# Sign of decoded weights by a parametric ReLU on ScalarE, and the feed-forward weights' low parts subtracted on VectorE: what it does to a one-core attention and gated-MLP kernel

## The chip, the cores and the metric

The kernel runs on one core of a Trainium2 chip. The metric is the device time of one execution in microseconds. A profile of one execution is at hand; its engines are TensorE (PE, and PEld for its weight loads), VectorE (DVE), ScalarE (ACT), GpSimd (POOL) and SyncE (SP), which here only issues DMAs.

## The reference, cut to what matters

All inputs are float64 in the host's arrays; the chip gets their bits and makes float32 of them.

```python
# attention in chunks of 64 tokens, batch 8, heads 8, 576 tokens, head_dim 64
attn = softmax(q_c @ k_c.T / 8) @ v_c
x = attn_out as (8, 576, 512)
# gated stage
gate = sigmoid(causal 5-tap depthwise convolution of x with conv_w)
x = (gate * (x @ w_val)) @ w_out
# feed-forward stage
xn = (x - mean) / sqrt(var + 1e-6) * g_ln
out = x + max(xn @ w_ch1, 0) @ w_ch2        # w_ch1 512x2048, w_ch2 2048x512
```

## The kernel before, in words

Tokens (4608) go in nine blocks of 512. The first stage runs attention and the gated stage block by block (`period`, in an order written out by hand for PE, DVE and ACT) and stores its result `y` in DRAM. The second stage first takes block 0 alone through the feed-forward layer (`ff1`, `ff2`, one step for each of the 16 slices f of 128 hidden columns), while the feed-forward weights are being loaded and decoded; after that the other eight blocks go in pairs (`ff_pair`, lines 597 to 660), with sums of weight slices that `make_pair` prepares.

Every matrix product is made of float32r operands in two parts, a high part and a low part, so each weight tile of 128x512 is needed as `hi` and `lo`. How a weight tile is made (`split`, line 103): the float64 tile is loaded into `raw` as two 32-bit words per number. `decode_copy` (line 87, ACT) reads the high words as if they were float32, multiplies by 2^-112 and writes `a` (tile `da`). `decode_bits` (DVE) shifts `a` left by 3 bits (line 91), which pushes the sign and the top exponent bits out, puts the sign bit of the high word back (line 92, inputs `raw` and `a`), and puts the top 3 bits of the low word in (line 93, inputs `raw` and `a`). `parts` makes `hi` as a copy of `a` rounded to float32r (line 100, ACT) and `lo` as `a - hi` (line 101, POOL).

There are 41 decodes: the convolution weights (20x128), four tiles of `w_val` and four of `w_out` in the first 60 us (`split_w`), and 32 tiles of `w_ch1` and `w_ch2`, two for each f (`split_ff`, called from `early_ff` for f below 4 and from `next_ff`, interleaved with `ff1` and `ff2`, for the rest). `ff_copy`, `ff_bits` and `ff_parts` (lines 709 to 722) are defined and never called. Tile `da` has three buffers in each of two pools, `raw` two in each; a tile of `raw` is free for the next load when line 93 has read it. For f of `w_ch1` the decoded tile is also stored to DRAM (line 147).

In the second stage only PE's order is written by hand; the order on DVE, ACT, POOL and SP is laid out by a planner ahead of time, from priorities and estimated durations, and each engine then works through its own list in order. On DVE the other work of that stretch is the low part `hl` of the hidden layer (line 455), layer norm (`ln_rows`, lines 411 to 423) and, at its end, the operands of the pairs (`right_operands`, lines 478 and 546). ACT has `hh` (line 454), the normalised rows (line 425), the evictions of transposes (line 435) and four square roots (line 416) beside lines 87 and 100.

Of the kernel before, what the change touches and what calls it, by code (L numbers as in the profile page):

```python
# [8 lines left out]
F32 = mybir.dt.float32  # L9
F32R = mybir.dt.float32r  # L10
U32 = mybir.dt.uint32
ACTF = mybir.ActivationFunctionType
ALU = mybir.AluOpType
# [6 lines left out]
def tile_chunk_attention_gated_mlp(ctx: ExitStack, tc: tile.TileContext, qk, v, w_val, conv_w, w_out, g_ln, w1, w2, out):  # L20
    nc = tc.nc
# [22 lines left out]
    scale = 1.0 / float(D) ** 0.5  # L44
# [39 lines left out]
        nc.sync.dma_start(out=t.rearrange("p c h d -> p (c h d)"), in_=v[u])  # L84

    def decode_copy(raw, a):
        nc.scalar.activation(out=a, in_=raw[:, :, 1].bitcast(F32), func=ACTF.Copy, scale=2.0 ** -112)

    def decode_bits(raw, a):
        lw, hw, au = raw[:, :, 0], raw[:, :, 1], a.bitcast(U32)  # L90
        nc.vector.tensor_scalar(out=au, in0=au, scalar1=3, scalar2=None, op0=ALU.logical_shift_left)
        nc.vector.scalar_tensor_tensor(out=au, in0=hw, scalar=0x80000000, in1=au, op0=ALU.bitwise_and, op1=ALU.bitwise_or)  # L92
        nc.vector.scalar_tensor_tensor(out=au, in0=lw, scalar=29, in1=au, op0=ALU.logical_shift_right, op1=ALU.bitwise_or)  # L93

    def decode(raw, a):
        decode_copy(raw, a)
        decode_bits(raw, a)

    def parts(hi, lo, a):
        nc.scalar.activation(out=hi, in_=a, func=ACTF.Copy)  # L100
        nc.gpsimd.tensor_tensor(out=lo, in0=a, in1=hi, op=ALU.subtract)  # L101

    def split(hi, lo, raw, pool=None):
        a = (pool or stg).tile([P, DM], F32, tag="da", name="da", bufs=3)
        decode(raw, a)
        parts(hi, lo, a)
        return a

    wv = {}
# [8 lines left out]
    def split_w(nm, c0=0, c1=CT):  # L118
        hs, ls = wv.setdefault(nm + "s", ([], []))
        for c, raw in list(enumerate(wv[nm]))[c0:c1]:  # L120
            hi = pD1.tile([P, DM], F32R, name=f"{nm}h{c}")
            lo = pD1.tile([P, DM], F32R, name=f"{nm}l{c}")
            split(hi, lo, raw)
            hs.append(hi)
            ls.append(lo)
# [13 lines left out]
    def split_ff(f, pool):  # L139
        r1, r2 = wraw.pop(f)  # L140
        g, m = divmod(f, NFA)
        if g in (0, 3):
            t = wA.tile([P, 2, DM], F32R, tag=f"s{NFA + m}", name="w0")
        else:
            t = p2[f"w{g}"].tile([P, 2, DM], F32R, tag=f"w{m}", name="w0")
        a = split(t[:, 0, :], t[:, 1, :], r1, pool)
        nc.sync.dma_start(out=a_dram[f], in_=a)
        w1s[f] = (t[:, 0, :], t[:, 1, :])
        t = (wA if f < NFA else p2["w"]).tile([P, 2, DM], F32R, tag=f"s{f}" if f < NFA else f"w1_{f}", name="w1")
        split(t[:, 0, :], t[:, 1, :], r2, pool)  # L150
        w2s[f] = (t[:, 0, :], t[:, 1, :])


# [555 lines left out]
    def ff_copy(k):  # L709
        a = fa[k] = stg.tile([P, DM], F32, tag="da", name="da", bufs=3)  # L710
        decode_copy(wraw[k // 2][k % 2], a)

    def ff_bits(k):
        decode_bits(wraw[k // 2][k % 2], fa[k])

    def ff_parts(k):
        f, a = k // 2, fa.pop(k)
        t = wA.tile([P, 2, DM], F32R, tag=f"s{f if k % 2 else NFA + f}", name="w1" if k % 2 else "w0")
        parts(t[:, 0, :], t[:, 1, :], a)
        (w2s if k % 2 else w1s)[f] = (t[:, 0, :], t[:, 1, :])  # L720
        if k % 2 == 0:
            nc.sync.dma_start(out=a_dram[f], in_=a)

    def early_ff(f):
        load_ff(f, stg)
        split_ff(f, stg)
# [194 lines left out]
    def next_ff(f):  # L921
        if NE <= f < NF:
            pool = stg2 if f % 2 else stg
            load_ff(f, pool)
            split_ff(f, pool)
# [95 lines left out]
```

## Time and profile before

| | |
|---|---|
| median of three runs | 1103.33 us (1102.24 to 1105.18) |
| profiled execution, its time | 1105.21 us |
| profiled execution, span of its instructions | 1103.4 us |
| PE busy | 1058.8 us (96%), granted clock 0.989 of full |
| DVE busy | 698.6 us (63%) |
| ACT busy | 499.6 us (45%) |
| POOL busy | 106.2 us (10%), of which line 101 57.8 us |
| chain that ended last | PE 79%, DVE 12%, ACT 3%, DMA 3% |

The 1.8 us between the profiled execution's time and its span lie around the instructions. Engine shares are means over the whole span; the stages differ, so the rows below take single stretches, in microseconds from the start of the span. The feed-forward weights are decoded from about 287 to 403 us.

### The profile page before, as it was taken

What the parts mean: (1) busy time and instruction counts of PE and PEld (TensorE: products, weight loads), DVE (VectorE), ACT (ScalarE), POOL (GpSimd) and SP (SyncE); (2) the same over time, 40 slices, a digit from 0 to 9 for tenths busy, and PEclk for the clock granted to TensorE, in tenths of its full rate; (3) what the DMA queues carried; (4) which work ended last, traced back from release to release, by engine and by line L of the source; (5) the groups of instructions that cost most, each with busy time, mean ns of one, the idle gap of its engine ahead of it and who ended that gap; (6) DMA issues with size and microseconds to landing.
All of it is one profiled execution on the core that took longest, in us unless ns stands there. A gap on an engine that the chain in (4) does not pass through costs nothing.

```text
span 1103.4 us, 16877 instructions
## 1 busy us (share of the span) xinstructions
PE 1058.8 (96%) x6778; PEld 862.9 (78%) x6778; DVE 698.6 (63%) x1107; ACT 499.6 (45%) x872; POOL 106.2 (10%) x120
## 2 busy tenths in 40 slices
PE   4899999999899898999999999999999999999998
PEld 3578888888677676888888888888888888888887
DVE  5899999997969987556638335448334447433434
ACT  5777777776756654344433233433233323222221
POOL 1210000000124444222200000000000000000000
PEclk9999999999999898999999999999999999999999
DMA  9534344412387745333335523323533224522211
GB/s 374 204 140 144 136 144 154 144 59 78 115 280 234 240 162 219 134 116 134 135 136 167 173 96 115 117 93 125 200 103 108 97 85 132 194 94 96 77 39 76
DMA packets 58725, 156.32 MB, mean 142 GB/s; under 512 B 5758, under 2 KB 13974, under 8 KB 56214
## 3 DMA queue, kind: packets, MB, share of 16 engines
q1 hardware_dynamic: 58646, 155.23, 40.7%
q8 instruction: 53, 0.87, 0.3%
q14 instruction: 26, 0.21, 0.1%
HBM read 117.46 MB, written 37.75 MB: 141 GB/s over the span
## 4 chain that ended last, share of the span: by engine, by line
PE 79%; DVE 12%; ACT 3%; DMA 3%; issue 2%; POOL 1%; SPq 0%; ACTq 0%; DVEq 0%; POOLq 0%
PE x L610 16%; PE acc L584 16%; PE psf L584 15%; PE zy L610 9%; PE pso L335 8%; PE psv L335 8%; PE sc L175 2%; PE x L250 2%; DVE da L92 2%; DVE h L622 2%; PE pst L218 1%; DMA qkr<-in_qk 1%; DVE da L93 1%; PE pst L433 1%; DVE xt L546 1%
## 5 line engine op out<-in xcount | busy, mean ns | idle before, releaser
L630 DVE TENSOR_TENSOR c<-x,c 128x512 f32<-128x512 f32 x96 | 66.2, 690 | 235.5 <-ACT c L626 179.6
L584 PE MATMUL acc<-w,h 128*128 128x512 f32 x768 | 184.5, 390 | 0.0
L584 PE MATMUL psf<-w,h 128*128 128x512 f32 x768 | 184.3, 389 | 0.0
L584 PEld LDWEIGHTS acc<-w,h 128*128 128x128 f32 x768 | 144.3, 188 | 30.1
L584 PEld LDWEIGHTS psf<-w,h 128*128 128x128 f32 x768 | 144.3, 188 | 29.8
L610 PE MATMUL x<-t,wc 128*128 128x512 f32 x576 | 149.0, 395 | 4.6 <-DVE c L630 4.6
L626 ACT ACTIVATE c<-zy 128x512 f32<-128x512 f32 x96 | 57.8, 602 | 185.2 <-PE zy L610 185.1
L610 PEld LDWEIGHTS x<-t,wc 128*128 128x128 f32 x576 | 109.3, 190 | 28.8 <-DVE c L630 6.2
L621 ACT ACTIVATE h<-c 128x512 fp32r<-128x512 f32 x96 | 60.6, 631 | 134.8 <-DVE c L630 134.2
L589 DVE TENSOR_TENSOR yt<-psf,yt 128x512 f32<-128x512 f32 x128 | 88.1, 690 | 23.5 <-PE psf L584 20.7
L304 DVE SCALAR_TENSOR_TENSOR cg<-xf,cw,cg 128x516 f32<-128x516 f32 (+1 forms) x136 | 100.4, 752 | 3.0
L610 PE MATMUL zy<-b,wc 128*128 128x512 f32 x384 | 99.1, 394 | 0.0
L610 PEld LDWEIGHTS zy<-b,wc 128*128 128x128 f32 x384 | 71.7, 189 | 14.4
L622 DVE SCALAR_TENSOR_TENSOR h<-c,h 128x512 fp32r<-128x512 f32 x96 | 68.0, 708 | 11.2 <-ACT h L621 10.9
L335 PE MATMUL pso<-oh,gh 128*128 128x512 f32 x144 | 58.3, 405 | 1.8 <-ACT gh L371 1.8
L335 PE MATMUL psv<-xh,vh 128*128 128x512 f32 x144 | 59.2, 411 | 0.0
L335 PE MATMUL pso<-oh,gl 128*128 128x512 f32 x144 | 56.9, 395 | 1.9 <-DVE gl L374 1.9
L101 POOL TENSOR_TENSOR w<-da,w 128x512 fp32r<-128x512 f32 x32 | 46.1, 1447 | 114.7 <-ACT w L100 108.7
L335 PE MATMUL pso<-ol,gh 128*128 128x512 f32 x144 | 56.6, 393 | 0.0
L335 PE MATMUL psv<-xl,vh 128*128 128x512 f32 x144 | 56.6, 393 | 0.0
L335 PE MATMUL psv<-xh,vl 128*128 128x512 f32 x144 | 56.6, 393 | 0.0
L621 ACT ACTIVATE h<-x 128x512 fp32r<-128x512 f32 x32 | 19.2, 598 | 81.3 <-PE x L610 81.3
(114 smaller groups left out, 1591.9 us busy)
## 6 DMA issues: line engine op xcount, KB each, us to landing
wc<-wc SPq DMA_DIRECT2D x112, 512.0 KB, 3.2
qkr<-in_qk SPq DMA_DIRECT2D x19, 1024.0 KB, 7.4
raw<-in_moe_w_ch SPq DMA_DIRECT2D x32, 512.0 KB, 4.4
vr<-in_v SPq DMA_DIRECT2D x18, 512.0 KB, 4.2
yd<-y SPq DMA_DIRECT2D x36, 256.0 KB, 2.0
out<-yt SPq DMA_DIRECT2D x36, 256.0 KB, 3.7
yr<-yd SPq DMA_DIRECT2D x32, 256.0 KB, 3.2
yt<-yd SPq DMA_DIRECT2D x32, 256.0 KB, 3.7
```

Source lines behind the costliest of these rows:

```text
L92: nc.vector.scalar_tensor_tensor(out=au, in0=hw, scalar=0x80000000, in1=au, op0=ALU.bitwise_and, op1=ALU.bitwise_or)
L101: nc.gpsimd.tensor_tensor(out=lo, in0=a, in1=hi, op=ALU.subtract)
L175: nc.tensor.matmul(out=ps[CH * c:CH * c + CH, par, g, :], lhsT=qt[r0:r0 + CH, hp, cs], rhs=kt[r0:r0 + CH, hp, cs], start=True, stop=True,)
L304: last_tap[j] = nc.vector.scalar_tensor_tensor(out=o, in0=xf[j][:, f, i:i + n], scalar=cw[:, i * CT + f:i * CT + f + 1], in1=o, op0=ALU.mu ...
L335: nc.tensor.matmul(out=ps, lhsT=lt, rhs=rh, start=(i == 0), stop=(i == n - 1))
L584: nc.tensor.matmul(out=ps, lhsT=lt, rhs=rh, start=(g == 0 and k == 0 and (first or half)), stop=(g == 1 and k == 2 and (last or half)),)
L589: nc.vector.tensor_tensor(out=yt[i], in0=ps, in1=yt[i], op=ALU.add)
L610: nc.tensor.matmul(out=ps, lhsT=lt, rhs=rh, start=(start and c == 0 and i == 0), stop=(c == 1 and i == 2), skip_group_check=True)
L621: nc.scalar.activation(out=t[:, 0, :], in_=src, func=ACTF.Relu)
L622: nc.vector.scalar_tensor_tensor(out=t[:, 1, :], in0=src, scalar=0.0, in1=t[:, 0, :], op0=ALU.max, op1=ALU.subtract)
L626: nc.scalar.activation(out=t, in_=zy, func=ACTF.Copy)
L630: nc.vector.tensor_tensor(out=t, in0=x, in1=t, op=ALU.add)
```

## The change

The activation of `decode_copy` becomes a parametric ReLU with slope 2^32 for negative inputs in place of a copy. The larger exponent of a negative number leaves a one in bit 31 after the shift by 3, so the instruction of line 92 is dropped, in all 41 decodes. `parts` takes the engine of the subtraction as an argument: GpSimd for `split_w`, VectorE for the 32 feed-forward tiles.

```diff
     def decode_copy(raw, a):
-        nc.scalar.activation(out=a, in_=raw[:, :, 1].bitcast(F32), func=ACTF.Copy, scale=2.0 ** -112)
+        nc.scalar.activation(out=a, in_=raw[:, :, 1].bitcast(F32), func=ACTF.Prelu, scale=2.0 ** -112, alpha=2.0 ** 32)
 
     def decode_bits(raw, a):
-        lw, hw, au = raw[:, :, 0], raw[:, :, 1], a.bitcast(U32)
+        lw, au = raw[:, :, 0], a.bitcast(U32)
         nc.vector.tensor_scalar(out=au, in0=au, scalar1=3, scalar2=None, op0=ALU.logical_shift_left)
-        nc.vector.scalar_tensor_tensor(out=au, in0=hw, scalar=0x80000000, in1=au, op0=ALU.bitwise_and, op1=ALU.bitwise_or)
         nc.vector.scalar_tensor_tensor(out=au, in0=lw, scalar=29, in1=au, op0=ALU.logical_shift_right, op1=ALU.bitwise_or)
...
-    def parts(hi, lo, a):
+    def parts(hi, lo, a, eng):
         nc.scalar.activation(out=hi, in_=a, func=ACTF.Copy)
-        nc.gpsimd.tensor_tensor(out=lo, in0=a, in1=hi, op=ALU.subtract)
-
-    def split(hi, lo, raw, pool=None):
+        eng.tensor_tensor(out=lo, in0=a, in1=hi, op=ALU.subtract)
+
+    def split(hi, lo, raw, pool=None, eng=nc.gpsimd):
...
-        a = split(t[:, 0, :], t[:, 1, :], r1, pool)
+        a = split(t[:, 0, :], t[:, 1, :], r1, pool, nc.vector)
...
-        split(t[:, 0, :], t[:, 1, :], r2, pool)
+        split(t[:, 0, :], t[:, 1, :], r2, pool, nc.vector)
...
-        parts(t[:, 0, :], t[:, 1, :], a)
+        parts(t[:, 0, :], t[:, 1, :], a, nc.vector)
```

## Rows read from the trace of the kernel before

**Rows 1.** The page's busy tenths, 40 slices of 27.6 us.

```profile
PE   4899999999899898999999999999999999999998
DVE  5899999997969987556638335448334447433434
```

**Rows 2.** Windows: stretch, length, busy us (instructions) by engine, clock, DMA share, GB/s.

```profile
40.00:62.00 22.00, 19.84 (x192) 12.91 (x191) 20.08 (x28) 15.04 (x22) 5.75 (x5) 1.00 0.39 135
62.00:254.00 192.00, 191.60 (x2475) 158.39 (x2476) 176.10 (x248) 138.63 (x190) 1.93 (x12) 0.99 0.37 129
...
290.00:313.00 23.00, 19.27 (x82) 15.15 (x81) 17.65 (x25) 15.89 (x35) 7.72 (x6) 0.93 0.61 199
313.00:417.30 104.30, 94.32 (x405) 75.78 (x405) 93.83 (x153) 63.38 (x126) 44.82 (x33) 0.95 0.67 219
417.30:440.00 22.70, 17.61 (x62) 12.83 (x61) 15.87 (x25) 9.08 (x20) 9.74 (x12) 0.85 0.70 266
```

**Rows 3.** PE's waits from 287 to 440 us: total us, times, longest.

```profile
PE x L610 <- DVE c L630: 4.6, 3, 2.6
PE pst L433 <- ACT xt L435: 3.4, 1, 3.4
PE psh L335 <- ACT w L100: 2.8, 1, 2.8
...
PE psh L335 <- DVE hl L455: 1.7, 1, 1.7
```

**Rows 4.** Groups on DVE, 287 to 403.5 us: busy us, mean ns, idle before.

```profile
L92 DVE SCALAR_TENSOR_TENSOR da<-raw,da 128x512 uint32<-128x512 uint32 x32 | 28.8, 904 | 0.4
L93 DVE SCALAR_TENSOR_TENSOR da<-raw,da 128x512 uint32<-128x512 uint32 x32 | 25.9, 813 | 0.3
L91 DVE TENSOR_SCALAR da<-da 128x512 uint32<-128x512 uint32 x32 | 17.3, 545 | 7.1 <-ACT da L87 7.1
...
L705 DVE TENSOR_TENSOR xn<-xt,xn 128x1024 fp32r<-128x1024 f32 x2 | 3.5, 1761 | 0.0
...
L374 DVE TENSOR_TENSOR gl<-gv,gh 128x512 fp32r<-128x512 f32 x4 | 2.7, 686 | 0.7 <-ACT gh L371 0.7
```

**Rows 5.** Tile da, whole span: ns minimum, median, maximum of each line.

```profile
L91 DVE TENSOR_SCALAR da<-da x40: 387/418/1472, 11.0 to 399.2; 128x512 uint32<-128x512 uint32 x40
L92 DVE SCALAR_TENSOR_TENSOR da<-raw,da x40: 650/692/1770, 11.4 to 399.9; 128x512 uint32<-128x512 uint32 x40
L93 DVE SCALAR_TENSOR_TENSOR da<-raw,da x40: 651/688/1670, 12.2 to 400.8; 128x512 uint32<-128x512 uint32 x40
...
L101 POOL TENSOR_TENSOR w<-da,w x32: 1278/1415/2213, 291.4 to 402.2; 128x512 fp32r<-128x512 f32 x32
```

**Rows 6.** Waits of SP's DMA queue, 287 to 417.3 us.

```profile
SPq L136 <- DVE da L93: 31.7, 12, 4.1
```

**Rows 7.** Timeline, 325 to 327.5 us: start, duration, instruction.

```profile
325.17 1.28 ACT L416 ACT_TABLE_LOAD   x1
325.22 1.54 POOL L101 TENSOR_TENSOR w<-da,w 128x512 fp32r<-128x512 f32 x1 [2.55 <-ACT w L100]
325.65 1.66 DVE L93 SCALAR_TENSOR_TENSOR da<-raw,da 128x512 uint32<-128x512 uint32 x1
...
326.46 0.21 ACT L416 ACTIVATE r<-ve 128x2 f32<-128x2 f32 x1
```

**Rows 8.** Groups on ACT, 287 to 440 us.

```profile
L87 ACT ACTIVATE da<-raw 128x512 f32<-128x512 f32 x30 | 19.9, 669 | 4.6 <-DMA raw<-in_moe_w_ch 4.6
...
L425 ACT ACTIVATE yr<-yr,w,r 128x512 f32<-128x512 f32 x8 | 6.2, 807 | 3.3 <-DVE w L423 3.3
...
L621 ACT ACTIVATE h<-c 128x512 fp32r<-128x512 f32 x3 | 1.9, 626 | 0.8 <-DVE c L630 0.8
L416 ACT ACT_TABLE_LOAD x1 | 1.3, 1283 | 0.0
...
```

**Rows 9.** DVE's waits, 287 to 417.3 us.

```profile
DVE da L91 <- ACT da L87: 7.1, 7, 1.9
```

More of the change, by code (lines that the diff above doesn't have):

```diff
@@ L97, in decode @@
         decode_bits(raw, a)
-    def parts(hi, lo, a):
+    def parts(hi, lo, a, eng):
         nc.scalar.activation(out=hi, in_=a, func=ACTF.Copy)
-        nc.gpsimd.tensor_tensor(out=lo, in0=a, in1=hi, op=ALU.subtract)
-    def split(hi, lo, raw, pool=None):
+        eng.tensor_tensor(out=lo, in0=a, in1=hi, op=ALU.subtract)
+    def split(hi, lo, raw, pool=None, eng=nc.gpsimd):
         a = (pool or stg).tile([P, DM], F32, tag="da", name="da", bufs=3)
         decode(raw, a)
-        parts(hi, lo, a)
+        parts(hi, lo, a, eng)
         return a
```

## Prediction

> **What bounds the kernel now.** First the page's busy tenths, to find the stages that are not simply TensorE at work. In [rows 1] PE stands at 9 in nearly every slice; it is lower in the first slices and in slices 10 to 15, and there DVE shows 9 as well, while after slice 16 DVE is at 3 to 5. So two places are open: the start, and the stretch in which the feed-forward weights are decoded. The table by windows puts sizes to them [rows 2]. From 62 to 254 us PE idles 0.4 us of 192: nothing done to another engine there can matter. From 313 to 417.3, the sixteen steps of block 0, PE is busy 94.3 of 104.3 us, so idle 10.0, and its granted clock is 0.95 of full. From 290 to 313 it idles 3.7 at a clock of 0.93. DVE is busy 93.8 of the 104.3, the nearest to PE of all others; ACT has 63.4.
>
> Then the list of PE's waits [rows 3]: 3.4 us in one wait for an eviction of a transpose (line 435) that stands on ACT behind weight copies, 2.8 us for a weight's high part (line 100), 1.7 us for `hl` (line 455), and after the stage 4.6 us for the sums of the first pair (line 630). The reader is to see that no wait is for a DMA, and that each of the first three hangs on the decode, directly or through the place in a queue.
>
> Last, what slows the decode. Undisturbed, line 92 takes 692 ns and line 93 688 (the medians), line 91 418 [rows 5]; in the stretch their means are 904, 813 and 545 [rows 4]. The timeline shows why [rows 7]: line 101 runs on POOL from 325.22 to 326.76, and line 93 on DVE, begun at 325.65, needs 1.66 us, ending 0.55 after POOL. The DMA queue follows DVE too: SP waited 31.7 us, in 12 waits, for line 93 to let go of a `raw` tile [rows 6]. So from about 290 to 417 us DVE with its delays by POOL paces the weights, and PE waits for them.
>
> **The change, part by part.**
>
> *Line 92 dropped.* 41 instructions go, 32 of them in the stretch, at 692 ns undisturbed: 22 us of DVE busy time there. The other nine lie before 62 us; there PE idles 2.2 us between 40 and 62 [rows 2], ACT and POOL have their own queues to work off, and I take 0 of it, with 2.2 as the other end.
>
> *The subtraction on DVE.* The trace has the same form, two float32 tiles of 128x512 in SBUF to a float32r tile: line 374, 686 ns [rows 4]. 32 of them are 22 us. So DVE's own work in the stretch stays as it was, to within 0.2 us.
>
> *POOL's share taken away.* What changes is the delay. Freed on DVE: line 92 32 x (904 - 692) = 6.8 us, line 93 32 x (813 - 688) = 4.0, line 91 32 x (545 - 418) = 4.1: together 14.9 us. Line 705, 128x1024, has two at a mean of 1761; twice line 374 bounds the undisturbed one at 1372, so at least 0.8 more. Layer norm's small instructions are left out. POOL keeps `make_pair`'s subtractions, which begin after 403 us, so the tail of the stretch keeps its delays.
>
> *The rule on the shared port.* In [rows 7] the later of the two instructions waited for the earlier to end. The Trainium skill, SBUF — State Buffer, "Who interferes with whom", states this: a VectorE instruction with two SBUF inputs, or in a two-port mode, and a GpSimd instruction that reads SBUF exclude each other for a whole instruction. This row agrees. By the rule alone each of the 32 subtractions could hold DVE for its full length, at 1278 ns or more 41 us; the sum above goes by the stretched means and has far less.
>
> *The latency of one weight.* From line 93 to PE it loses 692 ns of line 92 and 1278 - 686 = 592 ns at the subtraction, 1.3 us in all.
>
> *The activation.* Prelu isn't in the trace. Below: line 621, a Relu from SBUF of the same size, 626 ns; above: line 425 with two per-partition operands, 807; line 87 now takes 669 [rows 8]. Nothing in the diff adds an operand per partition, so I take 669, difference 0. The upper end adds 0.14 x 32 = 4.4 us to ACT, which has 40 us idle in the stretch.
>
> *The new wait.* DVE now has to wait for the high part (line 100) before it can subtract, and behind that subtraction stand all of DVE's later instructions: `hl` for PE, lines 91 and 93 of the next tiles, layer norm for ACT. POOL waited there at no cost. The nearest row is DVE's other wait for ACT in the same chain, line 91 behind line 87: 7.1 us over 32 tiles, 0.22 us each [rows 9]. I take the same, 7.1 us on DVE. Below stands 0 (two or more tiles are in work at once, so something else can be put between); above, the case of the rivals.
>
> *What PE gets back.* Of the 3.4 us wait I take 2.5 (the eviction stands behind copies that wait for line 93), of the 2.8 all (its chain holds a stretched line 93, a line 92 and POOL's subtraction), of the 1.7 all, of the remaining 10.0 - 7.9 = 2.1 us of idle time between 313 and 417.3 half, 1.0. From 290 to 313 only the stretched line 705, 1.1. That makes 9.1 us. TensorE's clock: stretches with idle gaps show 0.93 to 0.95, a mix of its levels of 2.4 and 1.2 GHz, the one without 0.99 [rows 2]; 5% of 94.3 us is 4.7 us, and if the gaps shrink about half of it should come back, 2.3. The new wait costs DVE 7.1 of the 14.9 us that are freed; so DVE is still 7.8 us better off, but I charge PE a third of it, 2.4. After 417.3 the 4.6 us stay, since line 630 waits in a stretch whose POOL work is untouched.
>
> Sum: 9.1 + 2.3 - 2.4 = 9.0 us. The profiled execution took 1105.2 and would take 1096.2; it lies 1.9 above the median of the runs, so for the median 1103.3 - 9.0 = 1094.3 us.
>
> **The rivals.**
>
> *Hidden or given back, 1100 to 1106.* The freed 14.9 us are used up if the 32 subtractions wait 0.47 us each, and the plan of DVE's queue changes with the edit, so gaps can open elsewhere. A DMA limit would do the same, but it is far: 104.3 us at 219 GB/s are 22.8 MB, and at the 266 GB/s of the next stretch [rows 2] they need 86 us, less than PE's own 94. For it: SP's queue is in order and waits behind DVE [rows 6].
>
> *DVE held up by ACT, slower.* Place: DVE at the subtraction, with line 100 still standing on ACT behind line 425 (0.81) or a string of line 435. If each subtraction waits for the high part and one more activation of that kind, some 0.63 + 0.6 = 1.2 us, DVE loses 38 us and wins 14.9: 23 more than before. It has 104.3 - 93.8 = 10.5 us to spare in the stretch, so PE would end it 12.6 us later: 1116 us. It decides from (14.9 + 10.5) / 32 = 0.8 us a wait on. Against it: ACT is only 61% busy there, and DVE's wait for line 87 has the same shape at 0.22.
>
> *The activation's table switches, slower.* Between 287 and 440 us there is one table load, for the square roots [rows 8], although Copy, Relu and Identity run there as well, so those run under the square root's table. If Prelu did not, each of the four square roots would need a load before and after it: seven more at 1.28 us, 9 us on ACT, and perhaps as many again before 62 us around the exponentials. Against the gain of 9.0 that gives 1094 to 1112, say 1106. Right behind the load in [rows 7] the next activation starts, at 326.46. The Trainium skill, ScalarE: Activation LUTs, "What ACT_TABLE_LOAD costs", counts a drain beside the load, 2.66 us a switch; by that the seven would be 19 us, an estimate from that page, and this case could reach 1131; the row shows no such drain. The page lists relu, copy, identity and abs as in every set, and doesn't say so of Prelu.
>
> *More than forecast.* All of the idle time and clock loss from 290 to 417.3 is 10.0 + 4.7 + 3.7 + 1.3 = 19.7 us; with two thirds or more of it gone the time is under 1090, at best 1084.
>
> **How the numbers follow.** A gain of 3.5 to 14 us: 0.60. More: 0.08. Hidden: 0.18. DVE held up: 0.10. Table switches: 0.04. What a measurement of this kernel can tell from no change is about 0.3%, 3.3 us: faster is the first two, 0.68; same 0.18; slower 0.14. The range runs from 1086, nearly all of the loss recovered, to 1105, the far side of the hidden case; the slower cases and a little at each end lie outside, about 2 in 10.
>
> **What would show it.** Lines 91 and 93 near 418 and 688 ns between 287 and 403 us; line 87 still near 670 and no table load beside it; POOL's busy time some 45 us less (32 x 1415 [rows 5]); the first product of the pairs starting near 408 us in place of 417.3; PE's idle time before it down to 2 or 3 us; on DVE a new wait for line 100 of about 7 us. The prediction is wrong if that wait is 20 us or more, if PE's waits for `hl` grow, or if table loads appear.

## The result, and the profile after

The changed kernel takes 1085.84 us, median of four runs (1085.06 to 1087.03), against 1102.89 for the kernel before in the same comparison: a ratio of 0.9843, 95% interval 0.9825 to 0.9860, or 17 us. The forecast was 1094.3 with a range of 1086.0 to 1105.0. The direction came as forecast, and so did the mechanism (VectorE freed of GpSimd's delay); the gain is nearly double the forecast, and the time lies 0.2 us below the range. Beside the experiments the changed kernel was timed once more: 1085.09 us, ratio 0.9825 (0.9807 to 0.9842). The profiled executions stand at 1105.2 and 1086.0 us, so 19 us apart; 1105.2 lies at the top of what the kernel before showed in that comparison (1102.24 to 1105.18).

The page's busy tenths of the kernel after, in 40 slices of 27.1 us, answer to [rows 1]:

```profile
PE   4899999999999997999999999999999999999998
DVE  5899999997958884555566344357344438333434
```

The dip of PE in slices 10 to 15 has shrunk to one slice, the last of them. DVE, at 9 in slices 10, 12 and 13 before, is at 9 in slice 10 alone.

The windows of the kernel after, with the columns of [rows 2]. The stage of the sixteen steps runs from its first product, at 309.6 us, to the first product of the pairs, at 398.9:

```profile
286.00:309.00 23.00, 20.47 (x80) 15.51 (x79) 15.53 (x25) 15.52 (x35) 0.00 (x0) 0.85 0.64 216
309.60:398.90 89.30, 88.38 (x406) 73.06 (x405) 76.78 (x156) 64.65 (x129) 7.06 (x7) 1.00 0.79 260
398.90:420.80 21.90, 16.02 (x66) 12.23 (x65) 12.83 (x26) 8.94 (x21) 10.69 (x14) 0.98 0.62 235
```

The stage is 89.3 us long where it was 104.3 [rows 2]. TensorE's idle time in it fell from 10.0 to 0.9 us and its granted clock rose from 0.95 to 1.00. VectorE is busy 76.8 us in place of 93.8: 17.0 less. Behind the stage TensorE idles 5.9 us of 21.9, about what it did (5.1 of 22.7).

PE's waits from 283 to 421 us, answering to [rows 3]:

```profile
PE x L609 <- DVE c L629: 3.4, 2, 2.7
PE x L609 <- DVE h L621: 2.4, 1, 2.4
PE pso L334 <- ACT gh L370: 1.7, 1, 1.7
PE pst L432 <- ACT yr L424: 0.9, 1, 0.9
```

Inside the stage one wait of 0.9 us is left; the waits for a transpose's eviction, for a weight's high part and for `hl` are gone.

The decode's groups on DVE, 283 to 390 us, answer to [rows 4] (line numbers are lower by one behind the dropped line: 92 here is line 93 before, 100 is line 101):

```profile
L92 DVE SCALAR_TENSOR_TENSOR da<-raw,da 128x512 uint32<-128x512 uint32 x32 | 22.0, 688 | 0.7 <-DVE w L422 0.2
L100 DVE TENSOR_TENSOR w<-da,w 128x512 fp32r<-128x512 f32 x32 | 21.7, 685 | 4.4 <-ACT w L99 4.1
L91 DVE TENSOR_SCALAR da<-da 128x512 uint32<-128x512 uint32 x32 | 13.4, 422 | 10.3 <-ACT da L87 10.1
```

The activation in ScalarE's groups, 283 to 421 us, answers to [rows 8]:

```profile
L87 ACT ACTIVATE da<-raw 128x512 f32<-128x512 f32 x30 | 19.9, 672 | 9.5 <-DMA raw<-in_moe_w_ch 6.5 <-issue 1.8 <-ACT w L99 0.9
```

The means are back at the undisturbed values, 688 and 422 ns; the subtraction costs 685; the parametric ReLU 672 where the copy took 669. VectorE's new wait for the high part is 4.1 us.

Layer norm's small instructions, which the prediction left out, were stretched too. One of four such lines, before and after:

```profile
L421 DVE TENSOR_SCALAR w<-w 128x2 f32<-128x2 f32 x4 | 2.8, 711 | 0.0
L420 DVE TENSOR_SCALAR w<-w 128x2 f32<-128x2 f32 x4 | 0.6, 155 | 0.0
```

The other three (lines 419, 422 and 423 before) fell from means of 424 to 430 ns to 152 to 156. The four together are 5.5 us of VectorE's time.

### The profile page after: what moved, and what is told of

It is laid out like the page before. It is cut to its first block, busy times and chain, and to the rows that moved or that the text cites. A ratio compares the mean times of both kernels' runs of the same rounds, so it can differ in the third digit from the quotient of the medians.

```text
span 1084.2 us, 16824 instructions
## 1 busy us (share of the span) xinstructions
PE 1050.2 (97%) x6778; PEld 857.8 (79%) x6778; DVE 672.2 (62%) x1098; ACT 499.4 (46%) x872; POOL 60.2 (6%) x88
## 4 chain that ended last, share of the span: by engine, by line
PE 85%; DVE 8%; DMA 2%; ACT 2%; issue 1%; POOL 0%; SPq 0%; ACTq 0%; POOLq 0%
PE acc L583 16%; PE x L609 16%; PE psf L583 15%; PE zy L609 10%; PE pso L334 8%; PE psv L334 8%; PE acc L469 4%; PE psh L334 3%; PE sc L174 2%; PE x L249 2%; DVE h L621 2%; DVE cg L303 1%; PE pst L432 1%; PE pst L217 1%; DMA raw<-in_moe_w_ch 1%
## 5 line engine op out<-in xcount | busy, mean ns | idle before, releaser
L609 PE MATMUL x<-t,wc 128*128 128x512 f32 x576 | 146.5, 390 | 3.4 <-DVE c L629 3.4
L477 POOL TENSOR_TENSOR wc<-raws,wc 128x256 fp32r<-128x256 f32 x56 | 45.4, 833 | 247.5 <-ACT wc L476 238.1
```

The lines of the kernel that those rows point to most:

```text
L477: eng.tensor_tensor(out=lo, in0=a, in1=hi, op=ALU.subtract)
L609: nc.tensor.matmul(out=ps, lhsT=lt, rhs=rh, start=(start and c == 0 and i == 0), stop=(c == 1 and i == 2), skip_group_check=True)
```

## The experiments

Each is timed against the kernel before on the same chip. That kernel's median was 1103.27 us in the first series, 1105.42 in the second and 1104.37 in the third, so ratios compare better across series than times. The edits are cut to the lines that matter, with comments added. An edit can also change the order in which the planner puts the instructions of an engine. TensorE's order is the same in all the traces; on VectorE and ScalarE the order is the changed kernel's in the two runs with GpSimd working beside, and differs somewhere in the other experiments.

**The first part alone.**

```diff
-        nc.scalar.activation(..., func=ACTF.Copy, scale=2.0 ** -112)
+        nc.scalar.activation(..., func=ACTF.Prelu, scale=2.0 ** -112, alpha=2.0 ** 32)
-        nc.vector.scalar_tensor_tensor(out=au, in0=hw, scalar=0x80000000, ...)      # line 92
```

> Only the first part of the change: parametric ReLU, the sign instruction of line 92 dropped in all 41 decodes, all subtractions still on GpSimd. Theory A, VectorE's budget: in the stretch of the feed-forward weights what counts is VectorE's work plus its delays against TensorE's own 89 us; 93.8 us less the 28.8 us of line 92 is 65, and even if every delay stays and moves to other instructions it is about 72, well under 89, so TensorE's idle time there goes and the time is 1084 to 1088 us, as with the whole change. Theory B, delay: each wait of TensorE comes from an instruction stretched by GpSimd; the stretching stays (lines 91 and 93 near 500 and 800 ns), so beside the 4 us at the start only 3 to 6 us come back: 1093 to 1096 us.

Measured: 1093.77 us, ratio 0.9904 (0.9881 to 0.9927). The window of the stage:

```profile
308.90:404.00 95.10, 90.49 (x405) 73.96 (x404) 76.02 (x129) 63.38 (x127) 40.91 (x32) 0.98 0.71 238
```

And two groups on DVE inside it:

```profile
L92 DVE SCALAR_TENSOR_TENSOR da<-raw,da 128x512 uint32<-128x512 uint32 x26 | 22.3, 863 | 0.5
L91 DVE TENSOR_SCALAR da<-da 128x512 uint32<-128x512 uint32 x26 | 16.3, 635 | 14.1 <-ACT da L87 14.1
```

VectorE is busy 76.0 us here and 76.8 in the whole change, yet the stage is 95.1 us long against 89.3. The budget theory falls with that: equal busy time, another length. What differs is where the 76 us come from, fewer instructions but stretched ones (863 and 635 ns), and that each low part still goes by way of GpSimd; in the list of waits TensorE waits in this stage for `hl` on VectorE (3.3 us) and a transpose's eviction on ScalarE (1.2), never for GpSimd. The profiled execution, 1089.46 us, is the fastest of its four (the others took 1093.68 to 1095.02), so a typical stage of this kernel may be longer.

**The second part alone.**

```diff
-        nc.gpsimd.tensor_tensor(out=lo, in0=a, in1=hi, op=ALU.subtract)
+        eng.tensor_tensor(out=lo, in0=a, in1=hi, op=ALU.subtract)      # nc.vector for the 32 feed-forward tiles
```

> Only the second part: line 92 and the copy stay, the 32 subtractions of the feed-forward weights move to VectorE. Theory A, budget: VectorE has 93.8 - 14.9 + 21.7 = 100.6 us of work where TensorE has 89, so the stretch stays near 101 to 104 us and the time is 1099 to 1103 us; nothing at the start. Theory B, delay: lines 91 to 93 fall to 418, 692 and 688 ns, the waits for stretched instructions go, and the stretch falls by some 10 to 13 us: 1090 to 1093 us. Rival of the prediction, VectorE held up by ScalarE: slower than before, 1106 us or more, with waits of VectorE for the high part of 20 us or more.

Measured: 1095.97 us, ratio 0.9919 (0.9899 to 0.9940), between the two expectations. The window of the stage:

```profile
309.20:409.10 99.90, 92.84 (x405) 75.13 (x404) 87.22 (x179) 62.79 (x125) 6.76 (x6) 0.96 0.72 240
```

VectorE's decode in it:

```profile
L101 DVE TENSOR_TENSOR w<-da,w 128x512 fp32r<-128x512 f32 x27 | 18.8, 702 | 1.0 <-ACT w L100 0.9
L93 DVE SCALAR_TENSOR_TENSOR da<-raw,da 128x512 uint32<-128x512 uint32 x26 | 18.2, 703 | 0.0
L92 DVE SCALAR_TENSOR_TENSOR da<-raw,da 128x512 uint32<-128x512 uint32 x26 | 17.5, 682 | 0.1
```

Nothing is stretched, but every weight passes one more instruction, and the stage is 10.6 us longer than with both parts, VectorE's busy time 10.4. So VectorE's own 22 us for line 92 cost something too, though it is idle 12.7 of the 99.9. The two parts give 9.5 and 7.3 us by medians, 16.8 together; the whole change gives 17.1. Within the intervals, some 2.5 us either way for each part, they add up. By the stages of the single profiles they give 9.2 and 4.4 of the 15.0, so how the gain splits between the two is known to a few microseconds only. The third theory in the expectation, VectorE held up by ScalarE, is out: its wait for the high part is 0.9 us.

**The first nine decodes alone.** Parametric ReLU and no line 92 in the first 60 us; the feed-forward tiles as before.

```diff
-        decode(raw, a)
+        decode(raw, a, sign)      # sign=True: the copy and line 92; for the 32 feed-forward tiles
```

> Parametric ReLU and no line 92 for the nine decodes of the first 60 us only; the 32 feed-forward tiles are decoded as before the change, with subtractions on GpSimd. If the 4.0 us by which the last product of the gated stage's first matrix came earlier belong to those nine decodes, the time falls by 3 to 5 us, 1098 to 1100, and the stretch of the feed-forward weights keeps its 104 us. Rival: those 4 us came from the planner's other order, through the feed-forward tiles whose first activations stand on ScalarE at 54 and 57 us; then 1102 to 1103.

Measured: 1102.24 us, ten runs from 1098.61 to 1105.20, ratio 0.9983 (0.9968 to 0.9997): by its time, the rival.

**The feed-forward tiles alone.** The complement: the first nine decodes with the copy and line 92.

```diff
-    def split(hi, lo, raw, pool=None, eng=nc.gpsimd):
+    def split(hi, lo, raw, pool=None, eng=nc.gpsimd, sign=True):      # False for the 32 feed-forward tiles
```

> The complement: the whole change for the 32 feed-forward tiles, the first nine decodes as before the change. If the two places add up, the stretch falls from 104 to 89 or 90 us and the time is 1102.9 less some 13 to 15, 1088 to 1090. Rival, the gain at the start hangs on the feed-forward tiles: 1085 to 1087.

Measured: 1087.32 us, ratio 0.9840 (0.9819 to 0.9860), between the two expectations; its stage takes 90.1 us. So the feed-forward tiles hold nearly the whole gain. What the start holds is less clear. In the tile view of `psv`, the gated stage's first product (duration minimum, median, maximum; first and last start in us), the four kernels before, after, first nine alone and feed-forward alone read:

```profile
L335 PE MATMUL psv<-xh,vh x144: 388/390/793, 49.3 to 294.5; 128*128 128x512 f32 x144
```

```profile
L334 PE MATMUL psv<-xh,vh x144: 389/389/501, 47.7 to 290.6; 128*128 128x512 f32 x144
```

```profile
L339 PE MATMUL psv<-xh,vh x144: 389/389/501, 47.9 to 290.9; 128*128 128x512 f32 x144
```

```profile
L339 PE MATMUL psv<-xh,vh x144: 389/389/793, 49.5 to 294.8; 128*128 128x512 f32 x144
```

Without line 92 at the start the last start comes 3.6 to 4.2 us earlier in these profiles. The other kernels' profiles have the same sign and more spread: 289.5 to 291.7 us where line 92 is dropped at the start and nothing else differs there, 293.6 for the second part alone, which keeps it. By medians those nine decodes are worth 1.0 us (the kernel with them alone), by its interval 0.3 to 3.5 us, and the kernel without them gives up 0 to 2 us against the two timings of the whole change. The profiles and the medians don't agree on this term, and it stays open.

**The changed kernel again.**

> The changed kernel once more, to have it beside the next runs on the same chip: 1084 to 1088 us.

Measured: 1085.09 us, ratio 0.9825 (0.9807 to 0.9842); stage 90.7 us, VectorE busy 77.1 in it. The next three runs are compared with it and with the first timing.

**The high part written twice.**

```diff
         nc.scalar.activation(out=hi, in_=a, func=ACTF.Copy)
+        if eng is nc.vector:
+            nc.scalar.activation(out=hi, in_=a, func=ACTF.Copy)
```

> The changed kernel with the high part of each of the 32 feed-forward tiles written twice by ScalarE, one after the other, so that VectorE's subtraction has to wait one activation of about 0.53 us longer each time, 17 us of ScalarE's time in all. It tests the wait for which the prediction charged TensorE 2.4 us. If VectorE's and ScalarE's spare time covers it, the time is within 1.5 us of the changed kernel, 1085 to 1088, though VectorE's waits for the high part grow from 4 us to 10 or more. Rival, the step of the prediction as it stood (a third of such waits is TensorE's): 4 to 6 us slower, 1090 to 1092.

Measured: 1090.92 us, ratio 0.9874 (0.9859 to 0.9888), so some 5 us slower: the rival's figure. PE's longest wait from 285 to 405.8 us:

```profile
PE pst L434 <- ACT xt L436: 5.2, 1, 5.2
```

VectorE's wait for the high part:

```profile
DVE w L102 <- ACT w L101: 7.6, 10, 1.2
```

VectorE's wait rose only from 4.3 to 7.6 us. TensorE's 5.2 us come in one wait for a transpose's eviction on ScalarE, behind the doubled copies. ScalarE's busy time rose by 15.5 us, and about a third of that reached the kernel's time; the waits that the list shows for it are on ScalarE's own queue and not through VectorE's wait. The edit also changed the planner's order on VectorE and ScalarE, the stage begins 3.7 us earlier (305.9) and is 10.6 us longer than the changed kernel's, so this run doesn't give the price of VectorE's wait by itself.

**GpSimd working beside, for nobody.** The changed kernel, and GpSimd subtracts each feed-forward tile as well, into a tile that is never read.

```diff
         eng.tensor_tensor(out=lo, in0=a, in1=hi, op=ALU.subtract)
+        if eng is nc.vector:
+            x = stg.tile([P, DM], F32, tag="x", name="x", bufs=1)
+            nc.gpsimd.tensor_tensor(out=x, in0=a, in1=hi, op=ALU.subtract)
```

> The changed kernel with a second subtraction of each feed-forward tile on GpSimd into a scratch tile that nobody reads: GpSimd works as much as before the change, but no weight waits for it. Theory B, delay: lines 91 and 92 of the changed kernel are stretched again to about 600 and 860 ns and the time rises to that of the parametric ReLU alone, 1091 to 1095 us. Rival: what the parametric ReLU alone lacked was the longer way of each weight through GpSimd, 0.6 us; then this stays at 1085 to 1088 us.

Measured: 1103.61 us, ratio 0.9989 (0.9979 to 0.9999). The gain is gone, and the time lies well above both expectations. Its windows before and in the stage:

```profile
285.00:313.30 28.30, 22.84 (x91) 17.32 (x90) 21.95 (x27) 16.92 (x37) 9.98 (x6) 0.82 0.53 183
313.30:416.20 102.90, 93.66 (x406) 76.23 (x405) 94.94 (x154) 63.50 (x126) 49.61 (x32) 0.95 0.65 216
```

The groups on DVE, 285 to 416.2 us:

```profile
L100 DVE TENSOR_TENSOR w<-da,w 128x512 fp32r<-128x512 f32 x32 | 32.3, 1015 | 4.2 <-ACT w L99 4.0
L91 DVE TENSOR_SCALAR da<-da 128x512 uint32<-128x512 uint32 x31 | 20.7, 669 | 7.2 <-ACT da L87 7.1
```

And on POOL:

```profile
L103 POOL TENSOR_TENSOR x<-da,w 128x512 f32<-128x512 f32 x32 | 51.7, 1617 | 111.2 <-ACT w L99 110.5
```

No instruction of PE, DVE or ACT waits for that subtraction in the list of waits; one DMA issue does, for 1.1 us. The trace shows the instructions of PE, DVE, ACT and SP in the same order as in the changed kernel, so another plan is no explanation either. Yet the subtraction on VectorE takes 1015 ns in place of 685 and line 91 669 in place of 421: 32 x 0.330 + 31 x 0.248 = 18.3 us of delay in these two lines, and the kernel is 18 us slower than the changed one in that series. That the two figures are equal is chance: other instructions are delayed too, and over the whole execution VectorE is busy 26.5 us longer than in the changed kernel (698.7 against 672.2). In the stage alone it is busy 18.2 us longer (94.9 against 76.8), and the stage is 13.6 us longer.

**Half of that.** The same over half of each tile.

```diff
-            nc.gpsimd.tensor_tensor(out=x, in0=a, in1=hi, op=ALU.subtract)
+            nc.gpsimd.tensor_tensor(out=x[:, 0:DM // 2], in0=a[:, 0:DM // 2], in1=hi[:, 0:DM // 2], op=ALU.subtract)
```

> As the run with GpSimd's unread subtraction beside, but over half of each tile (128x256), so that GpSimd holds VectorE about half as long. VectorE has 13 us to spare in the stretch of the changed kernel (76.8 busy of 89.9). Theory A': delays cost nothing until that is used up; half of the 18.7 us of delay is under it, so 1085 to 1088 us. Theory B, delay: what a weight or a product's low part has to wait is on TensorE's way each time, so about half of the 18 us come back: 1092 to 1097 us.

Measured: 1090.59 us, ratio 0.9882 (0.9867 to 0.9897), between the two expectations. The window of the stage:

```profile
310.10:404.60 94.50, 91.57 (x406) 75.22 (x405) 83.89 (x155) 63.28 (x126) 33.19 (x32) 0.96 0.73 239
```

The groups on DVE, 285 to 404.6 us:

```profile
L100 DVE TENSOR_TENSOR w<-da,w 128x512 fp32r<-128x512 f32 x32 | 25.8, 815 | 4.2 <-ACT w L99 4.1
L91 DVE TENSOR_SCALAR da<-da 128x512 uint32<-128x512 uint32 x31 | 15.9, 516 | 8.1 <-ACT da L87 8.0
```

The order of the instructions is again the changed kernel's. The delay of these two lines is 32 x 0.130 + 31 x 0.095 = 7.1 us, and the kernel is some 5 us slower than the changed one (0.9882 against 0.9843 and 0.9825). In the stage VectorE is busy 7.1 us longer and the stage is 5.2 us longer. So delay costs well before the 12.5 us for which VectorE idles in the changed kernel's stage are used up. Each microsecond that VectorE was busy longer cost the stage about 0.7 us, at 7 us as at 18; against the second profile of the changed kernel (90.7 us, VectorE 77.1) it is 0.6 and 0.7.

**Further moves off GpSimd.** The pairs' low parts on VectorE; the first eight tiles' low parts on VectorE; both.

```diff
-            high_low(wtiles[n][:, m, 0, :], wtiles[n][:, m, 1, :], a, nc.gpsimd)
+            high_low(wtiles[n][:, m, 0, :], wtiles[n][:, m, 1, :], a, nc.vector)
...
-    def split(hi, lo, raw, pool=None, eng=nc.gpsimd):
+    def split(hi, lo, raw, pool=None, eng=nc.vector):
```

> The changed kernel with the low parts of the pairs' weights (make_pair, 56 subtractions of 128x256) on VectorE as well, so that GpSimd has nothing left after 60 us. Delay theory: right_operands and the sums of the first pairs are no longer stretched, and of the 5.9 us that TensorE idles in the 22 us after the first product of the pairs 1 to 3 come back: 1083 to 1085 us. Rival: VectorE, in order, now waits there for ScalarE's high parts in front of line 629, for which TensorE waits: 1087 to 1091 us.

> The changed kernel with the subtractions of the first eight weight tiles on VectorE as well. Delay theory: some of the instructions stretched between 12 and 56 us (norm's product, line 91 at 1.4 and 1.5 us, the first gated low part at 1.58) get shorter, and ScalarE no longer waits for GpSimd to free a tile: 1082 to 1085 us. Rival: VectorE's order is written by hand there, and each subtraction stands right behind the decode and waits for ScalarE's copy: 1086 to 1092 us.

> All subtractions of weights on VectorE, first tiles, feed-forward tiles and pairs: GpSimd has only fills and halo copies left. If both of the last moves are free the time is 1082 to 1085 us; if the hand-written order at the start makes VectorE wait, 1086 to 1092.

Measured: 1084.63 us, ratio 0.9825 (0.9797 to 0.9854), for the pairs; 1087.50, 0.9856 (0.9840 to 0.9873), for the first tiles; 1086.24, 0.9841 (0.9819 to 0.9864), for both. None is faster than the change, at 0.9843 and 0.9825, by more than its interval. DVE's waits up to 62 us, with the first tiles moved:

```profile
DVE vl L100 <- ACT vh L99: 3.9, 4, 1.1
DVE ol L100 <- ACT oh L99: 2.6, 2, 1.9
```

Where VectorE's order is written by hand, with the subtraction right behind the decode, it does wait for ScalarE: 6.5 us over eight tiles, 0.8 us each. Over the 32 feed-forward tiles of the changed kernel it is 0.13 us each. What the longer waits cost in time is within the intervals.

## Why the prediction was off in size

**Right.** What bounds the kernel: the open stretch, VectorE and its delays in it. That the moved subtraction costs what line 92 cost, and the gain is the delay: VectorE's busy time in the stage fell by 17.0 us where 14.9 were counted and layer norm's part, 5.5 us, left out. The activation, 672 ns for 669 taken, one table load in the stretch as before. GpSimd's busy time fell by 46.0 us for 45. The new wait, 4.1 us where 7.1 were taken. The waits behind the stage stayed (4.6 us before, 5.8 after). The table switches and VectorE held up by ScalarE didn't come.

**The step that failed is "What PE gets back".** It went wait by wait and took shares: 2.5 of 3.4 us, half of the rest of the idle time, half of the clock, and charged a third of VectorE's new wait. For the stage that made 2.5 + 2.8 + 1.7 + 1.0 + 2.3 - 2.4 = 7.9 us. Measured were 15.0 (104.3 to 89.3): 9.1 of the 10.0 us idle came back, and 5.9 us of TensorE's busy time where the step had counted 4.7 for the whole loss by the clock. The loss was sized nearly right; the shares were guesses, and they left half of it standing. The charge for the new wait was too much as well: TensorE idles 0.9 us in the whole stage of the changed kernel, and the one wait listed there is for ScalarE, so VectorE's 4.1 us of waiting cost it at most that, where 2.4 were taken. What the runs show in place of the shares: with GpSimd's work put back beside, for nobody and in the same order of instructions, 13.6 of the 15.0 us are lost again, and with half of it 5.2. Read so, the loss was one, that of a stage which VectorE's delays set, and not a set of separate waits of which each keeps a part. Why about 0.7 us of each microsecond of delay reaches TensorE while VectorE still idles for 8 to 12 us of the stage isn't shown. The case "more than forecast" describes what happened, with a chance of 0.08.

**Line 92 was booked at nothing in the stretch,** since the subtraction takes its place on VectorE. In sum that is so. But the two parts alone, 9.5 and 7.3 us by medians, show that both have a price of several microseconds: one more instruction for each tile costs the stage about as much as the delay by GpSimd, as far as the intervals and the part of the start in the 9.5 us let one tell.

**Smaller terms.** The start was taken at 0 with 2.2 as the other end; it is 0 to 4 us, and open as the experiments left it. From 290 to 313 us 1.1 was taken for the stretched line 705; from the last of these `psv` products to the stage's first it was 18.6 us and is 19.0, so nothing came back, although VectorE's line there takes 1222 ns now. After the stage nothing was taken and 0.8 us came.

**The rule on the shared port.** The Trainium skill, SBUF — State Buffer, "Who interferes with whom", gives the exclusion, and by it alone 41 us could have been lost to 32 subtractions. In the run with GpSimd working for nobody VectorE lost 26.5 us and the kernel 18. The trace agrees with the mechanism, and the amount has to be read from the stretched means.

## What to carry to other kernels

An instruction whose result nobody waits for can still hold up the engine beside it: look for groups whose mean stands well above their median, multiply by their count, and test by running the neighbour's work for nobody. Once an engine paces a stage, the stage pays for a good part of its delays even where its busy share leaves room (here about 0.7 of each microsecond, with VectorE idle for a seventh of the stage); sum the whole loss of the stage (idle time and clock) and ask whether anything is left that would keep part of it, before shares are taken wait by wait. A wait put on an in-order engine is short where a planner can put other work in front of it (0.13 us here) and longer where the order is fixed right behind its producer (0.8 us). An experiment whose edit leaves the order of every other engine as it was, like the two with GpSimd beside, says more than one in which the plan changes too.

## What the runs showed of the hardware

The parametric ReLU runs between exponentials, sigmoids and square roots without a table load of its own (19 loads before and 19 after) and costs what a copy costs, 672 against 669 ns for 128x512. Behind 11 of the 19 loads before, the next activation starts 11 or 12 ns after the load's end; behind the others it waited for data. Thirty-two GpSimd subtractions that nobody reads cost the kernel 18 us out of 1085, nearly all that the change had won, and they hold up small instructions of VectorE too: one line of 128x2 elements had a mean of 711 ns beside GpSimd's subtractions and 155 without them.
